# Performer attention with two MoE layers: a block's slot, the last PSUM sums and the splitting of float64 weights

## The chip, the cores and the metric

The kernel runs on one NeuronCore of a Trainium2 chip. The metric is the device time of one execution in microseconds, from launch to the last store.

## The reference

Inputs: q, k, v of 4 batches x 8 heads x 576 tokens x 64, omega of 128 x 64, and the weights of two layers, w_a, w_b (512 x 1536), w_out (1536 x 512), w_in2 (512 x 2048) and w_out2 (2048 x 512). The weights arrive as float64.

```python
def phi(x):
    proj = np.einsum('bhsd,md->bhsm', x, omega)
    h = proj - np.sum(x * x, axis=-1, keepdims=True) / 2.0
    return np.exp(h - np.max(h, axis=-1, keepdims=True)) / np.sqrt(m)
...
num = np.einsum('bhsm,bhmd->bhsd', q_p, kv)
den = np.einsum('bhsm,bhm->bhs', q_p, z)[..., None] + 1e-06
x = (num / den)                      # 2304 tokens x 512
...
x = ((x @ w_a) * (x @ w_b)) @ w_out  # first layer
h = np.maximum(x @ w_in2, 0.0)
out = (h * h) @ w_out2               # second layer
```

## The kernel before

Every matrix operand is kept as a pair of fp32r values, a high half and a low half, and each product is three matmuls (`TERMS`: high x high, high x low, low x high). The work has three stages, all in one program.

**Attention and phase A (0 to some 655 us).** Lanes of attention steps (`k_lane`, `q_lane`) and the passes of the first layer (`a_units`) are emitted interleaved. For each of 12 blocks f of 128 hidden columns, a pass multiplies x by w_a and w_b (L636) and, after `gs`, by w_out (L661). The weights are made once, in the first passes: `get_w` loads a pair of w_a and w_b as 128 x 1024 float64 values, that is two int32 words each, into one of two buffers `raw`; `get_wo` does so for a 128 x 512 piece of w_out and stores the finished pair to `wo_d`, from which later passes load it. `load_split` keeps a load waiting for a few steps, then calls `split` (L166). There are 12 splits of each size. In `split`, `up` is the upper word and `u` the lower one of each float64:

- ACT scales the upper word as a float into `a` (L179), and turns the top 16 bits of the lower word into a number in place, in `raw` (L180).
- DVE makes the float32 value p, cut to its upper mantissa bits, out of `a` by a shift, a mask and the sign (L183, L187). ACT casts p to the high half (L191).
- DVE joins the remaining bits in `raw` (L192), takes the exponent of p into `a` (L196) and multiplies the two into the low half (L200).

`raw` has two buffers, `a` and `p` (the pool `cut`) one each.

**The first half of the second layer (some 655 to 825 us).** It is done by a scheme of seven products on 2 x 2 blocks (`in_step`), whose squared relu h*h goes to DRAM, `s_d[g]`, in four blocks a11, a12, a21, a22 (numbers 0 to 3) for each of three groups g of 768 tokens.

**The second half (`out_phase`, some 825 us to the end).** For each group seven products (`OUTS`) are summed in PSUM: in order X of a11, Y of a22, X of a12, W of a22, Y of a11, W of a12, Y of a21, each with its own block of weights, each over eight steps k. `sq_load` brings a block from `s_d` into one of five slots, `SQ_AT`: 0 is in area AB, 1 and 2 in area F, 3 and 4 in area T. F is also where the stage before keeps its results until they are stored; T is opened over that stage's areas. `prep(n)` makes the operand of step n, `LA` = 4 steps ahead: ACT casts the block to the high half (L1091), DVE subtracts for the low half (L1092, W<-F, W<-T or W<-AB by the block's slot), and from some products on DVE replaces a block by a sum or difference of two (`tt`, L1076). Five buffers `SOP_AT` in W take the operands in turn. Behind each product the PSUM sums are evicted (L1152 on DVE, L1157 on ACT). The loads just ahead of `out_phase` are issued on one queue in the order of the code:

```python
    sq_load(2, 0, 1)      # slot 2 (in F) <- group 0, block 1 (a12)
    sq_load(3, 0, 2)      # slot 3 (in T) <- group 0, block 2 (a21)
    op_load(T1)
```

In the last product of the last group, the three tiles t of 128 tokens are done one after the other, eight steps each, and each is evicted and stored at once (L1139). All three lie in one PSUM tile [128, 4, 256].

The order of the instructions on each engine is set by a scheduler from dependences, not by the code alone.

Of the kernel before, what the change touches and what calls it, by code (L numbers as in the profile page):

```python
# [8 lines left out]
F32 = mybir.dt.float32  # L9
F32R = mybir.dt.float32r  # L10
I32 = mybir.dt.int32
U32 = mybir.dt.uint32
U16 = mybir.dt.uint16
ACTF = mybir.ActivationFunctionType
ALU = mybir.AluOpType
AXX = mybir.AxisListType.X
# [5 lines left out]
TERMS = ((0, 0), (0, 1), (1, 0))  # L22
# [5 lines left out]
WORD_SCALE = 2.0 ** -111  # L28
# [8 lines left out]
def f32(ap):  # L37
    return ap.bitcast(F32)


def i32(ap):
    return ap.bitcast(I32)
# [3 lines left out]
def kernel(  # L46
# [13 lines left out]
    nc = tc.nc  # L60
# [53 lines left out]
    TH, NG = 384, NT // 768  # L114
    NJ = FB // 2
# [6 lines left out]
    def seg(name, off, *shape):  # L122

        n = 1
        for d in shape:
            n *= d
        t = area[name][:, off // 4:off // 4 + n]
        if len(shape) == 1:
            return t
        names = "abcdef"[:len(shape)]  # L130
        return t.rearrange(
            f"p ({' '.join(names)}) -> p {' '.join(names)}",
            **{c: d for c, d in zip(names[1:], shape[1:])},
        )
# [35 lines left out]
    def split(raw, t):  # L170

        n = raw.shape[1]
        up = raw[:, :, :, 1]
        u = raw[:, :, :, 0]
        a = top["cut"].tile([128, 2, 512], F32, tag="a", name="a")[:, 0:n]
        p = top["cut"].tile([128, 2, 512], F32, tag="p", name="p")[:, 0:n]
        nc.scalar.activation(out=a, in_=f32(up), func=ACTF.Copy, scale=WORD_SCALE)  # L179
        nc.scalar.activation(  # L180
            out=u, in_=raw.bitcast(U16)[:, :, :, 1], func=ACTF.Copy, scale=2.0 ** 7,
        )
        nc.vector.tensor_scalar(  # L183
            out=i32(p), in0=i32(a), scalar1=3, scalar2=0x7FFFF000,
            op0=ALU.logical_shift_left, op1=ALU.bitwise_and,
        )
        nc.vector.scalar_tensor_tensor(  # L187
            out=i32(p), in0=i32(a), scalar=-0x80000000, in1=i32(p),
            op0=ALU.bitwise_and, op1=ALU.bitwise_or,
        )  # L190
        nc.scalar.copy(out=t[:, :, 0, :], in_=p)  # L191
        nc.vector.scalar_tensor_tensor(  # L192
            out=u.bitcast(U32), in0=up.bitcast(U32), scalar=23, in1=u.bitcast(U32),
            op0=ALU.logical_shift_left, op1=ALU.bitwise_or,
        )
        nc.vector.tensor_scalar(  # L196
            out=i32(a), in0=i32(p), scalar1=-0x00800000, scalar2=None,
            op0=ALU.bitwise_and,
        )
        nc.vector.scalar_tensor_tensor(  # L200
            out=t[:, :, 1, :], in0=u.bitcast(U32), scalar=2.0 ** -43, in1=a,
            op0=ALU.mult, op1=ALU.mult,
        )


# [818 lines left out]
    def sq(slot):  # L1024
        return seg(*SQ_AT[slot], NJ, TH)

    def sq_load(slot, g, q_, j0=0, j1=8):
        nc.sync.dma_start(out=sq(slot)[:, j0:j1], in_=s_d[g][:, q_, j0:j1])
# [30 lines left out]
    ISC = 1.0 / W_SCALE  # L1059

    def out_phase():
        slots = {0: 0, 3: 1, 1: 2, 2: 3}
        free = 4
        loaded = {}
        sp1, rr, u1, sp5, c11 = (seg("T", 24576 + 3072 * x, 3, 256) for x in range(5))
        todo = [(g, i, k) for g in range(NG) for i in range(7) for k in range(NJ)]
        maps = [slots]
        for g in range(1, NG):
            m = maps[-1]
            maps.append({0: free, 3: m[3], 1: m[0], 2: m[1]})  # L1070
            free = m[2]
        sops = {}
        LA = len(SOP_AT) - 1

        def tt(o, x, y, op):
            nc.vector.tensor_tensor(out=o, in0=x, in1=y, op=op)  # L1076

        def prep(n):
            g, i, k = todo[n]
            m = maps[g]  # L1080
            a11, a12, a21, a22 = (sq(m[x])[:, k] for x in range(4))
            if i == 4:
                tt(a11, a22, a11, ALU.subtract)
            if i == 5:
                tt(a12, a12, a11, ALU.subtract)
            src = sq(m[OUTS[i][1]])[:, k]
            if n >= len(todo) - NJ:
                sop = seg("W", 43008 + 3072 * k, 2, TH)
            else:
                sop = seg(*SOP_AT[n % len(SOP_AT)], 2, TH)  # L1090
            nc.scalar.copy(out=sop[:, 0], in_=src)  # L1091
            nc.vector.tensor_tensor(out=sop[:, 1], in0=src, in1=f32(sop[:, 0]), op=ALU.subtract)  # L1092
            sops[n] = sop
            if i == 2:
                tt(a22, a21, a22, ALU.add)
            if i == 3:
                tt(a21, a11, a21, ALU.subtract)
            if g + 1 < NG and k == NJ - 1:
                nm = maps[g + 1]
                if i == 0:  # L1100
                    sq_load(nm[0], g + 1, 0)
                if i == 4:
                    sq_load(nm[3], g + 1, 3)
                if i == 5:
                    sq_load(nm[1], g + 1, 1)
                    sq_load(nm[2], g + 1, 2)

        def block(p, n, b, k, t, fresh):
            w = seg(*OP_AT[b][k], 2, 256)
            for s_, m_ in TERMS:  # L1110
                nc.tensor.matmul(  # L1111
                    p[:, t], lhsT=sops[n][:, s_, 128 * t:128 * t + 128], rhs=w[:, m_, :],
                    start=(fresh and k == 0 and t % 2 == 0 and (s_, m_) == TERMS[0]),
                    stop=(k == NJ - 1 and t > 0 and (s_, m_) == TERMS[-1]),
                    skip_group_check=True,
                )

        for n in range(LA):
            prep(n)
        ps = {}  # L1120
        for n, (g, i, k) in enumerate(todo):
            c, _, b = OUTS[i]
            if k == 0 and (c not in ps or ps[c][1] != g):
                tag = f"Y{g % 2}" if c == "Y" else c
                ps[c] = (psb.tile([128, 4, 256], F32, tag=tag, name=f"o{c}"), g)
                fresh = True
            elif k == 0:
                fresh = False
            p = ps[c][0]
            if n + LA < len(todo):  # L1130
                prep(n + LA)
            if n >= len(todo) - NJ:
                if k < NJ - 1:
                    continue
                for t in range(3):
                    for x in range(NJ):
                        block(p, n - NJ + 1 + x, b, x, t, False)
                    for o, d1 in ((sp1, 0), (sp5, 1)):
                        nc.vector.scalar_tensor_tensor(  # L1139
                            out=o[:, t], in0=p[:, t], scalar=ISC, in1=o[:, t],  # L1140
                            op0=ALU.mult, op1=ALU.add,
                        )
                        store(g, 1, d1, o, (t,))
                return
            for t in range(3):
                block(p, n, b, k, t, fresh)
            if k < NJ - 1:
                continue
            p = p[:, 0:3]

            def stt(o, sc, y):
                nc.vector.scalar_tensor_tensor(  # L1152
                    out=o, in0=p, scalar=sc, in1=y, op0=ALU.mult, op1=ALU.add
                )

            if i == 0:
                nc.scalar.mul(out=sp1, in_=p, mul=ISC)  # L1157
            elif i == 1:
                stt(rr, -ISC, sp1)
            elif i == 2:  # L1160
                nc.scalar.mul(out=c11, in_=p, mul=ISC)
                store(g, 0, 0, c11)
            elif i == 3:
                nc.scalar.mul(out=sp5, in_=p, mul=ISC)
                tt(sp5, rr, sp5, ALU.add)
            elif i == 4:
                stt(u1, ISC, rr)
            elif i == 5:
                stt(u1, ISC, u1)
                store(g, 0, 1, u1)  # L1170
            else:
                stt(sp1, ISC, sp1)
                store(g, 1, 0, sp1)
                stt(sp5, ISC, sp5)
                store(g, 1, 1, sp5)
# [67 lines left out]
    lanes, n = start_lanes()  # L1243
# [15 lines left out]
    side, n_side, done, u = iter(()), 0, 0, 0  # L1259
# [60 lines left out]
    psb = ctx.enter_context(tc.tile_pool(name="psb", bufs=1, space=bass.MemoryType.PSUM))  # L1320
# [25 lines left out]
    rst.close()  # L1346
    open_area("Q", 9216, F32R, "right")
    open_area("T", 39936, F32, "right")
    sq_load(2, 0, 1)
    sq_load(3, 0, 2)  # L1350
    op_load(T1)
    op_load(T2)
    op_load(B22)
    op_load(T3)
    out_phase()


# [31 lines left out]
```

## Time and profile before

| | us |
|---|---|
| median of 3 runs | 1023.91 |
| lowest and highest | 1022.79, 1028.66 |
| the profiled execution | 1023.56 |
| its span, first to last instruction | 1021.8 |
| PE, DVE, ACT, POOL busy | 987.2, 679.0, 551.3, 29.7 |

The profile is of one execution. PE is the matmul engine and PEld its weight loads, DVE the vector engine, ACT the scalar engine, SPq the queue that issues transfers. A group is given as "line engine operation out<-in", with the shape of one, its count, the busy time in us and the mean of one in ns; behind the last bar stands the idle time just before, with what ended it. PEclk is the granted clock of TensorE as a share of its full 2.4 GHz. Names such as T, F, W, AB are the areas in which the operands lie; oX, oY, oW are PSUM sums of `out_phase`, ps_p those of the attention's projections.

### The profile page before, as it was taken

How to read it: one execution, taken by the hardware profiler on the slowest of the kernel's cores; microseconds unless marked ns; L12 is line 12 of the kernel's file. 1: busy time of each engine (PE TensorE's matmuls, PEld its weight loads, DVE VectorE, ACT ScalarE, POOL GpSimd, SP SyncE). 2: the span in 40 equal slices, each digit the busy share in tenths (PEclk: the TensorE clock that was granted, in tenths of full speed). 3: DMA queues.
4: the chain of work that ended last, by engine and by line, in shares of the span. 5: the costliest groups of instructions: out<-in, count | busy, mean ns of one | idle time of the engine just before them, and what ended most of it. 6: DMA issues, size and time to landing. Idle time of an engine off the chain costs nothing.

```text
span 1021.8 us, 17357 instructions
## 1 busy us (share of the span) xinstructions
PE 987.2 (97%) x6337; PEld 902.3 (88%) x6337; DVE 679.0 (66%) x1651; ACT 551.3 (54%) x1305; POOL 29.7 (3%) x54
## 2 busy tenths in 40 slices
PE   4899999999999999999999999999999998999997
PEld 3789989999988887788888888899999998999997
DVE  4798796575655544443434999978776448697893
ACT  4986766564445553243333545767766544545561
POOL 3100101000000000000000000000000000000000
PEclk9999999999999999999999999999999998999999
DMA  6855865663452111232115999157595599514201
GB/s 170 243 154 181 271 224 155 195 215 115 140 170 70 55 55 55 67 94 72 54 61 165 328 329 330 42 175 241 172 293 197 208 407 419 204 56 167 82 17 47
DMA packets 110501, 171.07 MB, mean 167 GB/s; under 512 B 27728, under 2 KB 83536, under 8 KB 107856
## 3 DMA queue, kind: packets, MB, share of 16 engines
q1 hardware_dynamic: 108880, 168.39, 49.3%
q0 software_dynamic: 1536, 1.58, 0.6%
q8 instruction: 50, 0.82, 0.3%
q14 instruction: 35, 0.29, 0.1%
HBM read 120.13 MB, written 49.81 MB: 166 GB/s over the span
## 4 chain that ended last, share of the span: by engine, by line
PE 86%; DVE 6%; DMA 4%; ACT 2%; issue 1%; SPq 1%; DVEq 0%; ACTq 0%
PE abw L636 18%; PE y L661 12%; PE pY L966 10%; PE oY L1111 8%; PE ab L636 7%; PE oX L1111 5%; PE oW L1111 5%; PE pW L966 5%; PE ps_n L508 3%; PE pX L966 2%; PE ps_kv L450 2%; PE ps_p L378 2%; PE ps_p L312 2%; PE ps_qt L501 1%; DMA raw<-in_moe_w_b_dram 1%; DMA raw<-in_moe_w_out_dram 1%
## 5 line engine op out<-in xcount | busy, mean ns | idle before, releaser
L636 PE MATMUL abw<-x_all,W 128*128 128x512 f32 x576 | 146.6, 398 | 0.0
L661 PE MATMUL y<-gs,wo 128*128 128x256 f32 (+1 forms) x720 | 142.8, 336 | 0.0
L636 PEld LDWEIGHTS abw<-x_all,W 128*128 128x128 f32 x576 | 105.5, 189 | 19.2
L661 PEld LDWEIGHTS y<-gs,wo 128*128 128x128 f32 x720 | 109.6, 190 | 9.5
L636 PE MATMUL ab<-x_all,W 128*128 128x256 f32 x576 | 88.1, 294 | 0.0
L636 PEld LDWEIGHTS ab<-x_all,W 128*128 128x128 f32 x576 | 75.8, 191 | 0.7
L636 PE MATMUL abw<-x_mid,W 128*128 128x512 f32 x288 | 73.1, 400 | 0.0
L636 PEld LDWEIGHTS abw<-x_mid,W 128*128 128x128 f32 x288 | 52.2, 189 | 9.8
L385 DVE CUSTOM_DVE_ANT_0 c<-ps_p,c 128x128 f32<-128x128 f32 x152 | 37.8, 287 | 32.5 <-ACT c L383 32.0
L1091 ACT CAST W<-F 128x384 fp32r<-128x384 f32 x72 | 36.1, 512 | 41.4 <-PE oX L1111 21.5
L1111 PE MATMUL oW<-W 128*128 128x256 f32 x432 | 52.8, 283 | 0.0
L1111 PEld LDWEIGHTS oW<-W 128*128 128x128 f32 x432 | 52.3, 192 | 0.0
L1092 DVE TENSOR_TENSOR W<-F,W 128x384 fp32r<-128x384 f32 x72 | 39.4, 557 | 15.2 <-ACT W L1091 14.9
L742 ACT CAST gs<-a_s 128x256 fp32r<-128x256 f32 x84 | 33.2, 408 | 26.7 <-DVE a_s L741 26.4
L1111 PE MATMUL oX<-W 128*128 128x256 f32 x324 | 42.7, 295 | 4.1 <-DVE W L1092 4.1
L966 PE MATMUL pY<-W,M 128*128 128x384 f32 x240 | 45.9, 335 | 0.7 <-ACT AB L674 0.7
L383 ACT COPY c<-ps_p 128x256 f32<-128x256 f32 x76 | 27.1, 370 | 35.7 <-PE ps_p L378 35.2
L1111 PEld LDWEIGHTS oX<-W 128*128 128x128 f32 x324 | 42.0, 204 | 4.3 <-DVE W L1092 4.3
L636 PE MATMUL ab<-x,W 128*128 128x256 f32 x288 | 43.4, 290 | 0.5 <-DVE x L576 0.4
L1091 ACT CAST W<-T 128x384 fp32r<-128x384 f32 x56 | 28.7, 512 | 27.7 <-PE oY L1111 12.8
L966 PEld LDWEIGHTS pY<-W,M 128*128 128x128 f32 x240 | 41.9, 188 | 1.2 <-ACT AB L674 1.2
L1111 PE MATMUL oY<-W 128*128 128x256 f32 x324 | 40.9, 284 | 1.7 <-DVE T L1139 1.7
(193 smaller groups left out, 2108.0 us busy)
## 6 DMA issues: line engine op xcount, KB each, us to landing
wo<-wo_d SPq DMA_DIRECT2D x60, 512.0 KB, 3.5
s_d<-F SPq DMA_DIRECT2D x24, 768.0 KB, 6.1
raw<-in_moe_w_out_dram SPq DMA_DIRECT2D x32, 256.0 KB, 4.6
raw<-in_moe_w_in_dram SPq DMA_DIRECT2D x16, 512.0 KB, 6.7
W<-wo_d SPq DMA_DIRECT2D x4, 2048.0 KB, 14.7
F<-s_d SPq DMA_DIRECT2D x5, 1536.0 KB, 7.9
raw<-in_moe_w_a_dram SPq DMA_DIRECT2D x12, 512.0 KB, 5.0
raw<-in_moe_w_b_dram SPq DMA_DIRECT2D x12, 512.0 KB, 6.2
```

Of the source, the lines that this page charges most:

```text
L312: nc.tensor.matmul(ps[:, 2 * x:2 * x + 2].rearrange("p h m -> p (h m)"), lhsT=s, rhs=OMZ.rearrange("p h m -> p (h m)"), start=True, stop=True,
L378: nc.tensor.matmul(ps[:, x].rearrange("p a m -> p (a m)"), lhsT=self.s[:, x, o:o + 128], rhs=OM.rearrange("p a m -> p (a m)"), start=True, ...
L383: nc.scalar.copy(out=c, in_=ps[:, :, 1, :])
L385: nc.vector.tensor_tensor_reduce(out=c[:, x, :], in0=ps[:, x, 0, :], in1=c[:, x, :], scale=1.0, scalar=3.0e38, op0=ALU.add, op1=ALU.min, a ...
L508: nc.tensor.matmul(pn[:, x, :], lhsT=t["qT"][:, x % 2 * len(g) + x // 2, :], rhs=kv[:, x % 2, :], start=True, stop=True,)
L636: nc.tensor.matmul(ps, lhsT=wv[:, s_, kc, :], rhs=x[..., kc, m_, :], start=(kc == 0 and (s_, m_) == TERMS[0]), stop=(kc == KC - 1 and (s_, ...
L661: nc.tensor.matmul(y_part(pi, f, c), lhsT=wo[pi, f][:, s_, c * 128:(c + 1) * 128], rhs=g[:, m_, :],  start=(f == f0 and (wide or c % 2 == ...
L742: nc.scalar.copy(out=g[:, 0, c], in_=a_s)
L966: nc.tensor.matmul(p, lhsT=w[:, s_, 128 * kk:128 * kk + 128], rhs=y[:, ai, kk, m_, :], start=(c not in seen and kk == 0 and (s_, m_) == TE ...
L1091: nc.scalar.copy(out=sop[:, 0], in_=src)
L1092: nc.vector.tensor_tensor(out=sop[:, 1], in0=src, in1=f32(sop[:, 0]), op=ALU.subtract)
L1111: nc.tensor.matmul(p[:, t], lhsT=sops[n][:, s_, 128 * t:128 * t + 128], rhs=w[:, m_, :], start=(fresh and k == 0 and t % 2 == 0 and (s_, m ...
```

## The change

It has three parts. In `split`, p becomes the float32 value with all its mantissa bits, the last three of them joined from the lower word; the low half is p less the high half, so the weights are float32 words cut off from float64. ACT's conversion of the lower word and DVE's mask of the exponent are gone. In `out_phase`, blocks 1 (a12) and 2 (a21) trade slots, and their first loads trade places: block 1 now goes to T, by the first of the two. In the last group, the sums Y lie in two PSUM tiles: tiles t = 0 and 2 of 128 tokens in one, t = 1 in the other, and an eviction of all three is made of two instructions.

```diff
-        up = raw[:, :, :, 1]
-        u = raw[:, :, :, 0]
...
-        nc.scalar.activation(out=a, in_=f32(up), func=ACTF.Copy, scale=WORD_SCALE)
-        nc.scalar.activation(
-            out=u, in_=raw.bitcast(U16)[:, :, :, 1], func=ACTF.Copy, scale=2.0 ** 7,
-        )
+        nc.scalar.activation(out=a, in_=f32(raw[:, :, :, 1]), func=ACTF.Copy, scale=WORD_SCALE)
         nc.vector.tensor_scalar(
-            out=i32(p), in0=i32(a), scalar1=3, scalar2=0x7FFFF000,
+            out=i32(p), in0=i32(a), scalar1=3, scalar2=0x7FFFFFF8,
             op0=ALU.logical_shift_left, op1=ALU.bitwise_and,
         )
...
+        nc.vector.scalar_tensor_tensor(
+            out=p.bitcast(U32), in0=raw[:, :, :, 0].bitcast(U32), scalar=29,
+            in1=p.bitcast(U32), op0=ALU.logical_shift_right, op1=ALU.bitwise_or,
+        )
         nc.scalar.copy(out=t[:, :, 0, :], in_=p)
-        nc.vector.scalar_tensor_tensor(
-            out=u.bitcast(U32), in0=up.bitcast(U32), scalar=23, in1=u.bitcast(U32),
-            op0=ALU.logical_shift_left, op1=ALU.bitwise_or,
-        )
-        nc.vector.tensor_scalar(
-            out=i32(a), in0=i32(p), scalar1=-0x00800000, scalar2=None,
-            op0=ALU.bitwise_and,
-        )
-        nc.vector.scalar_tensor_tensor(
-            out=t[:, :, 1, :], in0=u.bitcast(U32), scalar=2.0 ** -43, in1=a,
-            op0=ALU.mult, op1=ALU.mult,
+        nc.vector.tensor_tensor(
+            out=t[:, :, 1, :], in0=p, in1=f32(t[:, :, 0, :]), op=ALU.subtract
         )
...
-        slots = {0: 0, 3: 1, 1: 2, 2: 3}
+        slots = {0: 0, 3: 1, 1: 3, 2: 2}
...
+        def tiles_of(p, t):
+            return p[0][:, t] if len(p) == 1 or t % 2 == 0 else p[1][:, 0]
...
-                    p[:, t], lhsT=sops[n][:, s_, 128 * t:128 * t + 128], rhs=w[:, m_, :],
+                    tiles_of(p, t), lhsT=sops[n][:, s_, 128 * t:128 * t + 128], rhs=w[:, m_, :],
...
+                        tags = ["Y0", "Y1"] if g == NG - 1 else [f"Y{g % 2}"]
+                    ps[c] = ([psb.tile([128, 4, 256], F32, tag=x, name=f"o{c}") for x in tags], g)
...
-    sq_load(2, 0, 1)
-    sq_load(3, 0, 2)
+    sq_load(3, 0, 1)
+    sq_load(2, 0, 2)
```

The lines of the changed program are shifted: L1092 of before is L1081 there, L1076 is L1065, L1152 is L1157, and in `split` L183, L187, L192 and L200 are answered by L177, L181, L185 and L190.

First place: DVE in `out_phase`, group 0, from the operands of the first Y product (W<-AB is the end of the X product, W<-F of before the Y product) to those of the second X product and its eviction of the Y sums (T<-oY). Before:

```order
L1092 TENSOR_TENSOR W<-AB,W 128x384 x3
L1092 TENSOR_TENSOR W<-F,W 128x384 x8
L1076 TENSOR_TENSOR F<-T,F 128x384 x4
L1152 SCALAR_TENSOR_TENSOR T<-oY,T 128x768
L1076 TENSOR_TENSOR F<-T,F 128x384 x4
L1076 TENSOR_TENSOR T<-AB,T 128x384 x2
L1092 TENSOR_TENSOR W<-F,W 128x384 x5
```

Now:

```order
L1081 TENSOR_TENSOR W<-AB,W 128x384 x3
L1081 TENSOR_TENSOR W<-F,W 128x384 x8
L1081 TENSOR_TENSOR W<-T,W 128x384 x4
L1157 SCALAR_TENSOR_TENSOR T<-oY,T 128x768
L1081 TENSOR_TENSOR W<-T,W 128x384 x4
L1065 TENSOR_TENSOR F<-F 128x384 x8
L1081 TENSOR_TENSOR W<-F,W 128x384
L1065 TENSOR_TENSOR F<-AB,F 128x384
```

The subtractions for the second X product (W<-F before, W<-T now) have moved ahead of the sums of two blocks, four of them ahead of the eviction; the eight sums now stand behind them in one piece, ahead of the subtraction for the next product.

Second place: DVE in the attention's opening, at the split of the second pair of weights (p, a, raw, W are of the split; ps_x, ps_p, ps_n, den of the attention). Before:

```order
L183 TENSOR_SCALAR p<-a 128x1024
L526 TENSOR_TENSOR x_all<-ps_x,x_all 128x256
L187 SCALAR_TENSOR_TENSOR p<-a,p 128x1024
L316 TENSOR_REDUCE nm<-ps_p 128x4
L192 SCALAR_TENSOR_TENSOR raw<-raw 128x1024
L196 TENSOR_SCALAR a<-p 128x1024
L482 TENSOR_SCALAR den<-ps_n 128x4
L200 SCALAR_TENSOR_TENSOR W<-raw,a 128x2x512
```

Now:

```order
L177 TENSOR_SCALAR p<-a 128x1024
L515 TENSOR_TENSOR x_all<-ps_x,x_all 128x256
L305 TENSOR_REDUCE nm<-ps_p 128x4
L181 SCALAR_TENSOR_TENSOR p<-a,p 128x1024
L305 TENSOR_REDUCE nm<-ps_p 128x4
L185 SCALAR_TENSOR_TENSOR p<-raw,p 128x1024
L305 TENSOR_REDUCE nm<-ps_p 128x4
L471 TENSOR_SCALAR den<-ps_n 128x4
L305 TENSOR_REDUCE nm<-ps_p 128x2
L474 RECIPROCAL den<-den 128x4
L190 TENSOR_TENSOR W<-p,W 128x2x512
```

Four instructions on wide operands remain of five, the last user of `raw` is the third of them, and five small ones of the attention stand between the second and the last, three of them between the join and the subtraction that reads ACT's high half.

Third place: PE at the end of the program, the last product's three groups of 24 matmuls; the number behind oY tells PSUM tiles apart. Before:

```order
L1111 MATMUL oY_10249<-W_100 128x256 x9
L1111 MATMUL oY_10249<-Q_8784,W_100 128x256 x12
L1111 MATMUL oY_10249<-M_6452,W_100 128x256 x3
L1111 MATMUL oY_10249<-W_100 128x256 [waits DVE_49]
L1111 MATMUL oY_10249<-W_100 128x256 x8
L1111 MATMUL oY_10249<-Q_8784,W_100 128x256 x12
L1111 MATMUL oY_10249<-M_6452,W_100 128x256 x3
L1111 MATMUL oY_10249<-W_100 128x256 [waits DVE_49]
```

Now:

```order
L1111 MATMUL oY_10201<-W_100 128x256 x9
L1111 MATMUL oY_10201<-Q_8736,W_100 128x256 x12
L1111 MATMUL oY_10201<-M_6404,W_100 128x256 x3
L1111 MATMUL oY_10202<-W_100 128x256 x9
L1111 MATMUL oY_10202<-Q_8736,W_100 128x256 x12
L1111 MATMUL oY_10202<-M_6404,W_100 128x256 x3
L1111 MATMUL oY_10201<-W_100 128x256 [waits DVE_49]
L1111 MATMUL oY_10201<-W_100 128x256 x8
```

The second group has no wait for DVE any more; the third, which writes the first group's PSUM tile again, keeps one, now a group of 24 matmuls behind the eviction for which it waits.

## Rows read from the trace of the kernel before

**Rows 1.** The page, busy time of each engine, share of the span, instructions.
```profile
PE 987.2 (97%) x6337; PEld 902.3 (88%) x6337; DVE 679.0 (66%) x1651; ACT 551.3 (54%) x1305; POOL 29.7 (3%) x54
```

**Rows 2.** Stretches: from:to, length, busy time of each engine, granted clock, DMA share, GB/s.
```profile
core 0: us, PE busy (x) PEld busy (x) DVE busy (x) ACT busy (x) POOL busy (x), PEclk, DMA share, GB/s
25.00:60.00 35.00, 30.63 (x210) 26.26 (x209) 28.66 (x55) 32.20 (x85) 4.50 (x7) 1.00 0.76 226
25.00:230.00 205.00, 196.36 (x1514) 185.02 (x1512) 157.45 (x377) 146.57 (x363) 18.90 (x31) 1.00 0.66 205
230.00:625.00 395.00, 394.38 (x2143) 329.06 (x2142) 219.09 (x713) 172.92 (x468) 2.34 (x4) 1.00 0.40 130
844.40:848.70 4.30, 0.23 (x2) 0.02 (x1) 4.27 (x9) 1.18 (x3) 0.00 (x0) 0.91 1.03 434
848.70:855.20 6.50, 6.48 (x32) 6.48 (x33) 5.65 (x12) 1.53 (x3) 0.00 (x0) 0.54 1.00 426
```

**Rows 3.** The chain that ended last, 835 to 860 us: start, us, what.
```profile
835.73 8.67 PE oY L1111 x70
...
844.43 0.04 DVE T L1152
...
845.30 1.96 DVE F L1076 x4
847.26 0.94 DVE T L1076 x2
848.20 0.48 DVE W L1092
...
848.72 11.28 PE oX L1111 x70
```

**Rows 4.** Timeline and transfers (KB each, us from issue to landing), 828 to 844 us.
```profile
828.76 1.23 SPq L1028 DMA_DIRECT2D T<-s_d  x1
...
T<-s_d SPq DMA_DIRECT2D x1, 1536.0 KB, 10.9
...
843.42 1.34 ACT L1091 CAST W<-F 128x384 fp32r<-128x384 f32 x3 [4.00 <-DMA F<-s_d]
...
835.82 0.42 SPq L1019 DMA_DIRECT2D W<-wo_d  x1
...
W<-wo_d SPq DMA_DIRECT2D x1, 2048.0 KB, 12.5
```

**Rows 5.** Waits of PE's loads, 1003 to 1019 us: total, times, longest.
```profile
PEld oY L1111 <- DVE T L1139: 2.1, 2, 1.1
```

**Rows 6.** The chain that ended last, 1000 us to the end.
```profile
1006.88 2.89 PE oY L1111 x24
...
1010.14 0.42 DVE T L1139
...
1010.61 3.15 PE oY L1111 x24
```

**Rows 7.** Groups of instructions by shape, in the split (550 to 790 us for the last).
```profile
L180 ACT ACTIVATE raw<-raw 128x1024 int32<-128x1024 uint16 x12 | 14.1, 1172 | 2.2 <-DMA raw<-in_moe_w_b_dram 2.2
L180 ACT ACTIVATE raw<-raw 128x512 int32<-128x512 uint16 x12 | 8.3, 691 | 1.7 <-DMA raw<-in_moe_w_out_dram 1.7
L191 ACT CAST W<-p 128x1024 fp32r<-128x1024 f32 x12 | 12.6, 1049 | 3.5 <-DVE p L187 3.5
L192 DVE SCALAR_TENSOR_TENSOR raw<-raw 128x1024 uint32<-128x1024 uint32 x12 | 14.7, 1221 | 1.8 <-ACT raw L180 1.8
L196 DVE TENSOR_SCALAR a<-p 128x1024 int32<-128x1024 int32 x12 | 8.4, 698 | 0.1
L196 DVE TENSOR_SCALAR a<-p 128x512 int32<-128x512 int32 x12 | 5.1, 423 | 0.1
L200 DVE SCALAR_TENSOR_TENSOR W<-raw,a 128x1024 fp32r<-128x1024 uint32 x12 | 14.6, 1217 | 0.1
...
L893 DVE TENSOR_TENSOR M<-AB,M 128x1024 fp32r<-128x1024 f32 x9 | 11.0, 1221 | 1.4 <-ACT M L890 1.4
```

**Rows 8.** Operations of line 312: least, median and longest ns, first and last start.
```profile
L312 PEld LDWEIGHTS ps_p<-OMZ,S x104: 186/190/338, 15.7 to 134.2; 128*128 128x128 f32 x104
L312 PE MATMUL ps_p<-OMZ,S x104: 377/379/797, 15.7 to 134.4; 128*128 128x256 f32 x104
```

More of the change, by code (lines that the diff above doesn't have):

```diff
@@ L1106, in prep, with parts_of @@
                     sq_load(nm[2], g + 1, 2)
+        def tiles_of(p, t):
+            return p[0][:, t] if len(p) == 1 or t % 2 == 0 else p[1][:, 0]
+        def parts_of(p, *aps):
+            if len(p) == 1:
+                return [(p[0][:, 0:3], *aps)]
+            return [
+                (p[0][:, 0:3:2], *(x[:, 0:3:2] for x in aps)),
+                (p[1][:, 0:1], *(x[:, 1:2] for x in aps)),
+            ]
         def block(p, n, b, k, t, fresh):
@@ L1111, in block @@
                 nc.tensor.matmul(
-                    p[:, t], lhsT=sops[n][:, s_, 128 * t:128 * t + 128], rhs=w[:, m_, :],
-                    start=(fresh and k == 0 and t % 2 == 0 and (s_, m_) == TERMS[0]),
-                    stop=(k == NJ - 1 and t > 0 and (s_, m_) == TERMS[-1]),
+                    tiles_of(p, t), lhsT=sops[n][:, s_, 128 * t:128 * t + 128], rhs=w[:, m_, :],
+                    start=(
+                        fresh and k == 0 and (t % 2 == 0 or len(p) == 2)
+                        and (s_, m_) == TERMS[0]
+                    ),
+                    stop=(k == NJ - 1 and (t > 0 or len(p) == 2) and (s_, m_) == TERMS[-1]),
                     skip_group_check=True,
@@ L1122, in out_phase @@
             c, _, b = OUTS[i]
[L1123 to L1128, printed above, removed]
+            if k == 0:
+                fresh = c not in ps or ps[c][1] != g
+                if fresh:
+                    if c != "Y":
+                        tags = [c]
+                    else:
+                        tags = ["Y0", "Y1"] if g == NG - 1 else [f"Y{g % 2}"]
+                    ps[c] = ([psb.tile([128, 4, 256], F32, tag=x, name=f"o{c}") for x in tags], g)
             p = ps[c][0]
@@ L1139, in out_phase @@
                         nc.vector.scalar_tensor_tensor(
-                            out=o[:, t], in0=p[:, t], scalar=ISC, in1=o[:, t],
+                            out=o[:, t], in0=tiles_of(p, t), scalar=ISC, in1=o[:, t],
                             op0=ALU.mult, op1=ALU.add,
@@ L1148, in out_phase @@
                 continue
-            p = p[:, 0:3]
             def stt(o, sc, y):
-                nc.vector.scalar_tensor_tensor(
-                    out=o, in0=p, scalar=sc, in1=y, op0=ALU.mult, op1=ALU.add
-                )
+                for x, o_, y_ in parts_of(p, o, y):
+                    nc.vector.scalar_tensor_tensor(
+                        out=o_, in0=x, scalar=sc, in1=y_, op0=ALU.mult, op1=ALU.add
+                    )
             if i == 0:
-                nc.scalar.mul(out=sp1, in_=p, mul=ISC)
+                nc.scalar.mul(out=sp1, in_=p[0][:, 0:3], mul=ISC)
             elif i == 1:
@@ L1160, in out_phase @@
             elif i == 2:
-                nc.scalar.mul(out=c11, in_=p, mul=ISC)
+                nc.scalar.mul(out=c11, in_=p[0][:, 0:3], mul=ISC)
                 store(g, 0, 0, c11)
             elif i == 3:
-                nc.scalar.mul(out=sp5, in_=p, mul=ISC)
+                nc.scalar.mul(out=sp5, in_=p[0][:, 0:3], mul=ISC)
                 tt(sp5, rr, sp5, ALU.add)
```

1 line of the change is left out of this document (removed).

## The prediction

> **What bounds the kernel now.** I read the page's line of totals first: PE is busy 987.2 of 1021.8 us, 97%, and DVE, the next, 66% [rows 1]. So a microsecond counts only where PE stands idle, or runs below full speed, and some 35 us is all that waits can give. The table of stretches says where that is [rows 2]. In each row the reader compares PE's busy time with the length of the stretch, and looks at the granted clock. From 25 to 230 us, where the attention's leftovers, the weights' splitting and phase A's first passes run together, PE lacks 205.0 - 196.36 = 8.6 us, half of it before 60 us (35.0 - 30.63 = 4.4), where ACT is busy for 32.2 of 35 us. From 230 to 625 us it lacks 0.6 us: nothing that the change does there to ACT or DVE can be felt. Around 844.4 us it lacks 4.1 us, and in the 6.5 us behind that the granted clock is 0.54 of full speed.
>
> The chain of waits tells that hole link by link [rows 3]. PE ends the first Y product at 844.4, and starts the second X product at 848.7. In between the chain lies on DVE: the rest of an eviction, four sums F<-T, two sums T<-AB, and only then the subtraction (0.48 us) that gives PE its next operand. DVE takes its instructions in order, and the sums stand ahead of the subtraction because ACT, which casts the operand first, got its source late: the transfer into F, issued behind one into T, landed at 843.4 (the cast's row: 4.00 us of idle ACT ended by "DMA F<-s_d") [rows 4]. The one into T was issued at 828.8 and took 10.9 us, so it had landed by 839.7.
>
> At the end, PE's loads wait twice for DVE, 1.1 us each time [rows 5]: between the three tiles of the last product it stands until DVE has read the tile that lies in the same PSUM tile as the next one. 24 matmuls take 2.89 us where nothing waits, and the chain shows an eviction of 0.42 us between two groups [rows 6].
>
> **The change, part by part.** *The slot.* The block of the second X product comes by the first transfer, into T, and that of a later sum by the second, into F. The second X product's first operands can then be cast from 839.7 on, 4.7 us before PE asks for them. In the new order, DVE's subtractions W<-T stand ahead of the eviction and ahead of the sums, so PE finds them done at 844.4: the 4.1 us go. With them goes the low clock that followed: the 70 matmuls of that product took 11.28 us, the 70 of the Y product before it 8.67 [rows 3], a difference of 2.6; the clock's row gives 6.5 x 0.46 = 3.0 [rows 2]. I take 2.8. What is late next: the sums for the third block now wait for F (843.4). Eight F<-F at 1.96 / 4 = 0.49 us are 3.9 us, and in the new order they stand between the subtraction for the product's last operand and that for the first of the next product. The former waits for a buffer that comes free with the product's third operand, 3 x 1.08 us behind 844.4 at 847.65; a cast and a subtraction (0.48 us each) later it is 848.6, behind the sums 852.5, and 853.0 to 853.2 when the next product's first operand is done. PE asks for it 8.65 us after 844.4, at 853.05. I cost that at nothing; it is 0.2 us if nothing covers it. The weights of the next product (T1) were issued at 835.8 and took 12.5 us, so they have landed at 848.3 [rows 4]; PE will want them at 853.05 instead of 860: covered. In the two later groups the same swap puts one load into the other area; there the loads lie far ahead of their use. Nothing. **-4.1 and -2.8.**
>
> *The tail.* With tiles 0 and 2 in one PSUM tile and tile 1 in another, the next group's matmuls have no eviction to wait for; the third group does go back to the first tile, but that was read while the second group ran (2.89 us against two evictions of 0.42). The last eviction and stores stay. The two waits go [rows 5]: **-2.1**. For it, two evictions of the last group are cut into two instructions each; an eviction of 256 columns takes 0.42 us [rows 6], so even if each cut cost a whole one of these, it would be 0.84 us. PE works on the next product meanwhile, with four operands prepared: at nothing.
>
> *The weights.* Per pair of w_a and w_b ACT loses one conversion of 1172 ns, per w_out one of 691 ns [rows 7]: 12 x 1.172 + 12 x 0.691 = 22.4 us, of the 146.6 that ACT is busy from 25 to 230 us. DVE loses the mask for the exponent, 698 ns and 423 ns: 12 x 1.121 = 13.5 of 157.5 us. The join of the words is again a scalar_tensor_tensor of the same width over uint32 (1221 ns then and now), and the last product (1217 ns) becomes a subtraction, whose nearest row, 128x1024 from float32 into fp32r elsewhere in the kernel, also has 1221 [rows 7]. Those two trades are at nothing. The raw slot is now read last by the third DVE instruction and not by the fifth, so the next weights' transfer may be issued earlier; and the cut tile that ACT writes first is free after DVE's second instruction. What is added is a wait: the low half now needs ACT's high half. Behind it on DVE stand the attention's reductions and small divisions, and in the new order they stand partly ahead of it, as the rows of the order show.
>
> What that gives PE, no row tells; so bounds. The most is all of its idle time from 25 to 230, 8.6 us. The least is a loss: in the opening stretch, where PE idles for ACT and DVE, two pairs are split, and if each low half there waits out a whole cast of the high half (1049 ns), that is 2 x 1.05 = 2.1 us lost. I take half of the 8.6, **-4.3**, since half of that idle time lies before 60 us where ACT is busy 92% of the stretch, and 15% of its work over the 205 us goes; the rest sits behind transfers and PE's own chain.
>
> The page named PE by its matmuls' busy time. In the Trainium skill, Perfetto Trace Analysis, section Identifying the Most-Contended Engine, it is said that matmul busy time is a poor measure since matmuls are pipelined, and that the busy time of weight loads tells the room. By it the sum would be some 6 us lower (third rival). The trace speaks against it here: a matmul of ps_p holds PE for 379 ns and its load for 190 [rows 8], so loads idle half the time there while PE has no gap.
>
> The sum: 4.1 + 2.8 + 2.1 + 4.3 = 13.3 us. The profiled execution took 1023.56 us, 0.35 below the median of the runs (1023.91): 1023.56 - 13.3 = **1010.3 us**. With the bounds of phase A: 1006.0 to 1016.7.
>
> **The rivals.** *Phase A gives nothing.* For it: from 60 to 230 us PE is busy 196.36 - 30.63 = 165.7 of 170 us, and a scheduler has set all engines' order anew, so a wait may only move. Against: ACT's load in the opening. Time: 1023.56 - 9.0 = 1014.6, up to 1016.7 with the loss above. 20%.
>
> *The hole moves.* DVE's eight F<-F sums (3.9 us) come at once and in one place; if ACT's casts there are late too, PE waits at the first W product as it did at the second X product, and the clock drops again. Then the 6.9 us come back: 1017.2. For it: the sums are queued ahead of a subtraction as before. Against: they start some 4 us before PE needs it, with four operands prepared. 8%.
>
> *PE has more room than its busy time shows.* Going by the loads, PE is idle 205.0 - 185.0 = 20.0 us between 25 and 230 [rows 2]; half of it gone would give 1023.56 - 9.0 - 10.0 = 1004.6. 7%, by the row against it above.
>
> *Slower: the low half's new wait.* ACT's queue is long there, and each low half waits in DVE's queue for a cast behind other ACT work, with PE's evictions behind it. If PE loses a whole cast at each of the splits, 1.05 us per pair and half of that per w_out, it is 12 x 1.05 + 12 x 0.53 = 19 us: 1023.56 - 9.0 + 19 = 1033.6. It decides from 9.0 / 24 = 0.38 us per split; below that the kernel isn't slower. For it: DVE is in order. Against: between the subtraction and the join DVE has other instructions, and PE has a lead. 4%.
>
> *It doesn't do what it says*: the tail still waits, and the hole stays (the cast's source was in time, but ACT's queue wasn't). Then only phase A's 4.3: 1019.3. 3%.
>
> **How the numbers follow.** The forecast has 58%, with 1006.0 to 1014.6 as its own range. For 8 in 10 the range takes in the rival of nothing from phase A, that of the moved hole with its clock, and the third, since the sizes within each are rough: 1004 to 1018.5. About 0.5%, 5.1 us, is what a measurement of this kernel can tell: faster means below 1018.8. Forecast, first and third rival and nearly all of the second lie there: 0.58 + 0.20 + 0.07 + 0.05 = 0.90, of which I give 0.02 away for what I have not thought of. Within it: 0.09; slower: 0.03.
>
> **What would show it.** Right: from 825 us on no wait of PE for W by DVE above 0.5 us and a clock of 1.00 behind the Y product; the second X product in 8.4 to 8.7 us; no wait of the last loads for T; ACT's busy time lower by 22 us, DVE's by 13; PE's idle time between 25 and 230 at 3 to 6 us. Wrong: a wait for DVE at the first W product, an idle time of 9 us or more before 230, or DVE waiting about 1 us for ACT's cast at each low half, with PE behind it.

## The result, and the profile after

The changed kernel takes 1014.05 us (median of 6 runs, 1010.27 to 1016.17); before took 1024.14 in the runs beside it. The ratio is 0.9894, 95% interval 0.9867 to 0.9922: 10.9 us less by the ratio, 10.1 by the two medians. The forecast was 13.3 us less, 1010.3, with 1004 to 1018.5 as its range. The profiled execution took 1015.39 us, its span is 1013.6.

The page's totals answer to [rows 1]. PE's busy time is the same, ACT has lost 19.2 us and DVE 11.2; the prediction's 22.4 and 13.5 us were sums of durations. The page counts stretches in which an instruction ran, and back-to-back instructions overlap a little there; that this is all of the difference is not shown:

```profile
PE 985.9 (97%) x6337; PEld 901.7 (89%) x6337; DVE 667.8 (66%) x1629; ACT 532.1 (52%) x1281; POOL 29.2 (3%) x54
```

The chain of waits behind 826 us answers to [rows 3] (start, us, what):

```profile
826.00 8.64 PE oX L1111 x72
...
836.52 8.64 PE oY L1111 x70
845.16 8.64 PE oX L1111 x72
853.80 8.64 PE oW L1111 x72
```

The Y product ends at 845.16 and the second X product starts there, where it stood until 848.72 before. It takes 8.64 us, not 11.28: the low clock is gone with the wait. The first W product follows without a gap too. At the end there is no row for a wait of the loads on T ([rows 5] had 2.1 us); what is left from 822 us on for PE's loads is the wait ahead of the first Y product, which before has as well:

```profile
PEld oY L1111 <- ACT W L1080: 1.5, 1, 1.5
PEld oY L1111 <- DVE W L1081: 0.3, 1, 0.3
```

So the last stage, from the first X product to the last instruction, takes 1013.6 - 826.0 = 187.6 us. Before it was 1021.8 - 825.22 = 196.6, by this row of before's chain:

```profile
825.22 8.64 PE oX L1111 x72
```

That is 9.0 us, the 4.1, 2.8 and 2.1 of the sum. What is missing is all in front of it: the first X product starts 0.8 us later than before, where 4.3 us earlier was forecast. (These are single executions. In the traces of e1, e3 and e4 below, whose order up to that product is before's, it starts at 826.33 to 826.66, so before's 825.22 is an early one.) The stretches say more (to be read beside [rows 2]):

```profile
core 0: us, PE busy (x) PEld busy (x) DVE busy (x) ACT busy (x) POOL busy (x), PEclk, DMA share, GB/s
25.00:60.00 35.00, 31.91 (x211) 27.11 (x212) 26.51 (x53) 27.93 (x84) 4.59 (x8) 1.00 0.72 214
150.00:153.00 3.00, 1.14 (x9) 0.73 (x7) 1.04 (x4) 2.42 (x5) 0.00 (x0) 1.00 1.05 353
153.00:158.00 5.00, 5.00 (x29) 4.97 (x30) 1.12 (x6) 1.31 (x5) 0.00 (x0) 0.66 0.65 219
25.00:230.00 205.00, 198.70 (x1524) 188.12 (x1525) 148.14 (x355) 129.86 (x346) 18.96 (x32) 0.99 0.65 201
```

PE's idle time from 25 to 230 us fell from 8.6 to 6.3. But of the 3 us from 150 on PE is idle for 1.9, and in the next 5 the granted clock is 0.66: 5 x 0.34 = 1.7 us of work lost. Outside this range PE is also busy for less: 10.81 us of the first 25 (11.72 before; its wait for the load of omega takes 3.9 us instead of 3.3), and 13.81 us from 640 to 655 (14.22 before). That accounts for the 0.8 us: 2.3 - 1.7 - 0.9 - 0.4 = -0.7. Of the six runs, two had a mean granted clock of 1.000 and 0.999 and took 1010.27 and 1011.27 us; the other four, the profiled one among them, had 0.998 and took 1013.07 to 1016.17.

In the kernel before, the same stretches have holes of 1.6 and 0.4 us, of which PE waits 1.5 us for DVE (xh, L486), and the clock stays at 1.00:

```profile
150.00:153.00 3.00, 1.41 (x10) 1.01 (x9) 2.88 (x5) 2.97 (x6) 0.00 (x0) 1.00 0.56 154
153.00:158.00 5.00, 4.61 (x38) 4.40 (x38) 4.24 (x17) 2.92 (x10) 0.00 (x0) 1.00 0.92 300
```

So the hole as such is not new; its cause is. In the changed kernel the chain of waits tells where it comes from:

```profile
145.23 0.45 PE ps_t L346 x4
...
145.70 0.38 SPq L326
...
146.12 5.32 DMA raw<-in_moe_w_b_dram
...
151.60 1.12 ACT a L176
152.72 0.16 ACT x L564
...
152.93 1.18 PE ab L625 x7
```

Read from the bottom: PE waits for a cast of x on ACT; that stands behind ACT's scaling `a` of the last pair of weights; this waits for w_b; and w_b's transfer was issued at 146.12, behind a load of wo and one of k (L326), which waited one after the other on the same queue for PE. Its partner w_a had gone out at 142.78. Both went out earlier than in the kernel before (153.27 and 153.71), but ACT's scaling of the pair has moved up as well, ahead of the cast. Another thing shows in the groups of the split (0 to 250 us):

```profile
L190 DVE TENSOR_TENSOR W<-p,W 128x1024 fp32r<-128x1024 f32 x12 | 14.7, 1221 | 3.2 <-ACT W L189 3.1
...
L190 DVE TENSOR_TENSOR wo<-p,wo 128x512 fp32r<-128x512 f32 x12 | 8.3, 690 | 5.5 <-ACT wo L189 5.4
```

DVE stands for 3.1 + 5.4 = 8.5 us ahead of the subtractions, until ACT has cast the high half: most of the 13.5 us that the missing mask gave it.

### The profile page after: what moved, and what is told of

It reads as the page before. It is cut to its first block, busy times and chain, and to the rows that moved or that the text cites. A ratio compares the mean times of both kernels' runs of the same rounds, so it can differ in the third digit from the quotient of the medians.

```text
span 1013.6 us, 17323 instructions
## 1 busy us (share of the span) xinstructions
PE 985.9 (97%) x6337; PEld 901.7 (89%) x6337; DVE 667.8 (66%) x1629; ACT 532.1 (52%) x1281; POOL 29.2 (3%) x54
## 4 chain that ended last, share of the span: by engine, by line
PE 82%; DVE 8%; DMA 4%; ACT 3%; issue 1%; SPq 1%; ACTq 0%; DVEq 0%
PE abw L625 13%; PE y L650 11%; PE pY L955 10%; PE ab L625 9%; PE oY L1111 8%; PE oW L1111 5%; PE oX L1111 5%; PE pW L955 5%; PE ps_n L497 3%; PE ps_p L301 3%; PE pX L955 2%; PE ps_kv L439 2%; PE ps_p L367 2%; DMA raw<-in_moe_w_b_dram 2%; PE ps_qt L490 1%
## 5 line engine op out<-in xcount | busy, mean ns | idle before, releaser
L625 PEld LDWEIGHTS abw<-x_all,W 128*128 128x128 f32 x576 | 105.5, 189 | 19.2
L1081 DVE TENSOR_TENSOR W<-F,W 128x384 fp32r<-128x384 f32 x72 | 39.6, 562 | 11.6 <-ACT W L1080 11.0
L1080 ACT CAST W<-T 128x384 fp32r<-128x384 f32 x56 | 28.5, 513 | 30.2 <-PE oY L1111 10.9
L625 PEld LDWEIGHTS ab<-x,W 128*128 128x128 f32 x288 | 39.2, 198 | 1.5 <-ACT x L564 1.5
L1111 PEld LDWEIGHTS oY<-W 128*128 128x128 f32 x324 | 39.8, 192 | 0.1
```

What stands on the lines that cost most here:

```text
L625: nc.tensor.matmul(ps, lhsT=wv[:, s_, kc, :], rhs=x[..., kc, m_, :], start=(kc == 0 and (s_, m_) == TERMS[0]), stop=(kc == KC - 1 and (s_, ...
L1111: nc.tensor.matmul(tiles_of(p, t), lhsT=sops[n][:, s_, 128 * t:128 * t + 128], rhs=w[:, m_, :], start=(fresh and k == 0 and (t % 2 == 0 or ...
```

## The experiments

Times are medians, compared with runs of the kernel before on the same chip (1025.08 beside e1 to e4, 1025.21 beside e5 to e8, 1024.23 beside e9 and e10, 1024.40 beside the last two). Since these differ, gains are compared by the ratios: 0.001 is 1.02 us.

**The three parts apart.** e1 is the changed kernel with before's `split`. e2 is the kernel before with the new `split` alone. e3 and e4 are the kernel before with one of the other parts:

```diff
# e3
-        slots = {0: 0, 3: 1, 1: 2, 2: 3}
+        slots = {0: 0, 3: 1, 1: 3, 2: 2}
...
-    sq_load(2, 0, 1)
-    sq_load(3, 0, 2)
+    sq_load(3, 0, 1)
+    sq_load(2, 0, 2)
# e4
-                tag = f"Y{g % 2}" if c == "Y" else c
+                        tags = ["Y0", "Y1"] if g == NG - 1 else [f"Y{g % 2}"]
```

> Before's splitting of the weights, with the new slot and the two PSUM tiles. Theory: the weights' part gave nothing, all of the gain is in the last stage: the stage in front as before (the first X product starts at 825.2 us), the last stage as in the changed kernel (187.6 us to the end): span 1012.8, time about 1014.6, level with the changed kernel within 2 us, and no low clock near 155 us. Rival: the weights' part gave its 4.3 us and the rest less: then this kernel takes 1018 or more.

> The new splitting alone, slot and PSUM tile as before. Theory: within 2 us of before (about 1024), PE's idle time from 25 to 230 us about 6 us instead of 8.6, and this given back by a stretch of low clock behind a hole near 151 us. Rival: 4 us faster, 1019 to 1020.

> The slot alone. By the sum: 4.1 us of wait and 2.8 of low clock go: 1024.1 - 6.9 = 1017.2; the two waits of 1.1 us at the end stay. Rival: the wait moves to the next W product and the clock falls there: 1022 or more.

> The two PSUM tiles alone. By the sum: 2.1 us, 1022.0; the wait of 4.1 us ahead of the second X product and the low clock stay. Rival: the two evictions cut in two cost what the tail gives: 1024.

| | us | ratio to before | 95% interval |
|---|---|---|---|
| e1 slot and tail | 1015.81 | 0.9907 | 0.9889 to 0.9925 |
| e2 weights alone | 1022.40 | 0.9969 | 0.9957 to 0.9982 |
| e3 slot alone | 1019.33 | 0.9939 | 0.9917 to 0.9962 |
| e4 tail alone | 1023.93 | 0.9984 | 0.9966 to 1.0002 |

The last stage can be read off each trace, from the first X product to the end of the span. The first rows of the chain there, of e1, e3 and e4, and the second X product of e4:

```profile
826.51 8.64 PE oX L1122 x72
```
```profile
826.66 8.64 PE oX L1111 x72
```
```profile
826.33 8.64 PE oX L1122 x72
...
849.82 10.15 PE oX L1122 x70
```

With spans of 1014.1, 1016.5 and 1019.6 us the stage takes 187.6, 189.8 and 193.3 us, against 196.6 before. The slot is worth 6.8 us (6.9 by the sum), and the tail 2.2 on top of it (2.1 by the sum). In e4, 1.1 of its 3.3 us are not the tail's: the second X product behind the same hole took 10.15 us instead of 11.28, the low clock having ended sooner. The timings of e3 and e1 agree with the traces. That of the tail alone does not tell: 1023.93 is its rival's number, and the interval holds both nothing and the 2.1 us; its ten runs lie between 1020.86 and 1027.92. What speaks for the tail is the stage in the traces, and e1 against e3. In e3 the loads' waits at the end are still there:

```profile
PEld oY L1111 <- DVE T L1139: 2.1, 2, 1.1
```

The weights' part gave 3.2 us alone (1.8 to 4.4), and beside the others 0.9907 - 0.9894, about 1.3 us, within the uncertainty of both (some 3.4 us either way). So the part gives something, which speaks against "nothing", and most likely less than the 4.3 of the forecast, which the timings alone do not rule out. Its trace (e2) has the hole and the low clock near 150 us too. So has that of e4, although it has before's split, and on PE, DVE and ACT up to 970 us the same instructions in the same order as the kernel before. Its holes are those of before, 1.6 and 0.4 us, and yet behind them:

```profile
153.00:158.00 5.00, 4.61 (x27) 4.59 (x26) 3.21 (x11) 1.65 (x4) 0.00 (x0) 0.66 0.91 292
```

Whether a hole of this size costs clock thus differs between executions of one order; the 1.7 us are what it cost in the profiled one.

**The hole near 151 us.** Two experiments move one row each in the changed kernel, with an order-only edge between two instructions; every row of PE and DVE stays where it was. In e5 the k load and a load of wo are issued behind the last w_b (ACT's scaling then moves up two rows); in e6 ACT's scaling of that pair stands one row later, behind the cast of x, and w_b is as late as before. In short (the names stand for the instructions; the first is put behind the second):

```diff
# e5
+    tc.add_manual_dep(k_load[10], w_b_load[11], NoSync)
+    tc.add_manual_dep(wo_load[6], w_b_load[11], NoSync)
# e6
+    tc.add_manual_dep(a_scale[11], x_cast[3], NoSync)
```

> The changed kernel with one difference: the transfer of the last w_b is issued right behind that of its w_a, ahead of a load of k (and of one of wo) that waits for PE. Theory: in the changed kernel w_b lands at 151.4 us behind that load, ACT's scaling of it holds up the cast of x behind it, PE stands 0.57 + 1.29 us and then runs at half clock until 157.7. Here w_b lands near 149.5, the second hole is under 0.5 us and the clock stays at 1.00: 1.1 + 1.8 us less than the changed kernel's 1014.05, about 1011. Rival: the stage is bound by PE's other work, and the time stays within 1 us of 1014.

> The changed kernel with one difference: on ACT the scaling of the last pair stands one row later, behind the cast of x that PE waits for; w_b is as late as before. Theory: the 1.29 us of waiting for the cast go and with them the low clock from 154 to 157.7: about 1011. Rival: the pair's split, now later, is what PE waits for next, or the clock falls for the 0.57 us that stay: 1013 to 1014.

Measured: e5 1011.92 us (0.9872, 0.9853 to 0.9891), e6 1012.19 (0.9869, 0.9851 to 0.9888); 2.3 and 2.6 us better than the changed kernel by the ratios, each within the uncertainty of such a difference, 3.4 us. In the traces the first X product starts at 822.96 and 823.61, 3.0 and 2.4 us earlier than in the changed kernel. ACT's rows of e6 (start, us, engine, line), w_b issued at 145.86:

```profile
151.18 0.27 ACT L569 CAST x<-ps_xt 128x128 fp32r<-128x128 f32 x1 [0.31 <-PE ps_xt L563]
151.40 1.14 ACT L181 ACTIVATE a<-raw 128x1024 f32<-128x1024 f32 x1
```

and its stretch, to be held against that of the changed kernel above:

```profile
150.00:153.00 3.00, 2.31 (x17) 1.87 (x16) 1.14 (x5) 2.38 (x5) 0.00 (x0) 1.00 1.03 347
153.00:158.00 5.00, 5.00 (x45) 5.00 (x43) 3.26 (x21) 4.08 (x14) 0.00 (x0) 1.00 0.58 210
```

PE is idle for 0.7 us of the three, and the clock stays. So w_b's landing hurts through ACT's order alone: w_b is not wanted yet, but what ACT does with it stands ahead of something that PE wants. From 25 to 230 us the two save 0.5 and 0.8 us of PE's idle time, and the rest is the low clock; their times are level with those two runs of the changed kernel that did without it (1010.27 and 1011.27). Without the hole the weights' part is worth 0.9907 - 0.9870, about 3.8 us.

**What of the weights' part counts.** e7 and e8 start from e1 and leave out one instruction of before's `split` each.

```diff
# e7
-        nc.scalar.activation(
-            out=u, in_=raw.bitcast(U16)[:, :, :, 1], func=ACTF.Copy, scale=2.0 ** 7,
-        )
# e8
-        nc.vector.tensor_scalar(
-            out=i32(a), in0=i32(p), scalar1=-0x00800000, scalar2=None,
-            op0=ALU.bitwise_and,
-        )
```

> The kernel of e1 (before's splitting with slot and tail) without ACT's conversion of the lower words, so that the low halves get wrong bits. Theory: what the weights' part gains in the opening comes from ACT's 22.4 us: PE's idle time from 25 to 60 us falls from 4.3 to about 3, the whole 2 to 3 us below e1 (1015.8), about 1013. Rival: it comes from DVE's five instructions becoming four: then this one stays within 1 us of 1015.8.

> The kernel of e1 without DVE's mask of the exponent, so that the low halves have a wrong scale. Theory: DVE's 13.5 us are not what PE waits for: idle time from 25 to 60 us stays near 4.3, time within 1 us of 1015.8. Rival: they are: 2 us less, 1013.5.

Measured: e7 1013.69 us (0.9885, 0.9867 to 0.9903), e8 1009.22 (0.9849, 0.9827 to 0.9872). Against e1 that is 2.3 and 5.9 us, the former within its uncertainty of 2.6. e7 came as expected. e8's theory, that DVE's 13.5 us are not what PE waits for, fell, and by more than its rival named: they are worth at least as much as ACT's 22.4. The stretches of e7, then of e8:

```profile
25.00:60.00 35.00, 32.70 (x222) 28.10 (x221) 30.21 (x59) 29.09 (x83) 4.56 (x8) 1.00 0.76 227
25.00:230.00 205.00, 200.47 (x1543) 188.95 (x1542) 160.03 (x385) 131.16 (x346) 18.61 (x32) 1.00 0.67 207
```
```profile
25.00:60.00 35.00, 33.50 (x231) 29.35 (x229) 27.90 (x54) 32.16 (x89) 4.87 (x8) 1.00 0.76 226
25.00:230.00 205.00, 201.81 (x1562) 191.56 (x1560) 150.54 (x372) 148.84 (x376) 18.88 (x32) 1.00 0.67 210
```

In e8 ACT is as busy as before (32.16 of 35 us), and yet PE is idle for only 1.5 us of the opening, where before had 4.4: ACT's busy share does not tell what it costs PE. The chain of waits tells more. In the kernel before all of PE's waits from 25 to 60 us end with ACT, 4.3 us in all, but from 30.5 to 36.9 us the chain runs over DVE and its split, the mask (L196) in it, and from there to ACT's next scaling; the conversion (L180) is not on it:

```profile
35.02 0.60 DVE a L196
35.62 0.07 DVE den L482
35.69 1.20 DVE W L200
36.89 0.02 issue
36.91 0.67 ACT a L179
```

In e8, without the mask, the conversion is on the chain:

```profile
32.42 1.18 ACT raw L180
```

Either instruction alone leaves PE less idle time (4.5 and 3.2 us from 25 to 230) than the change does, which drops both (6.3). Both kernels got another order from the scheduler, too, so a part of the difference is the order's.

**The low half's wait.** That the change adds a wait of DVE for ACT was the next suspect. In e9 the low half is p less p, and nothing waits for the cast. In e10 ACT casts p before the last bits are joined, and the join goes to `a`:

```diff
# e9
-            out=t[:, :, 1, :], in0=p, in1=f32(t[:, :, 0, :]), op=ALU.subtract
+            out=t[:, :, 1, :], in0=p, in1=p, op=ALU.subtract
# e10
+        nc.scalar.copy(out=t[:, :, 0, :], in_=p)
         nc.vector.scalar_tensor_tensor(
-            out=p.bitcast(U32), in0=raw[:, :, :, 0].bitcast(U32), scalar=29,
+            out=a.bitcast(U32), in0=raw[:, :, :, 0].bitcast(U32), scalar=29,
             in1=p.bitcast(U32), op0=ALU.logical_shift_right, op1=ALU.bitwise_or,
         )
-        nc.scalar.copy(out=t[:, :, 0, :], in_=p)
         nc.vector.tensor_tensor(
-            out=t[:, :, 1, :], in0=p, in1=f32(t[:, :, 0, :]), op=ALU.subtract
+            out=t[:, :, 1, :], in0=a, in1=f32(t[:, :, 0, :]), op=ALU.subtract
         )
```

> The changed kernel, with the low half made as p less p instead of p less the high half (it becomes zero, so the product lacks it): same instructions and shapes, but DVE no longer waits for ACT's cast. Theory: in the changed kernel DVE stood 3.1 us ahead of the twelve wide subtractions and 5.4 us ahead of the twelve narrow ones for that cast, 8.5 of the 13.5 us that the missing mask had given back; without it the weights' part gives as much as the mask alone did in e8 (1009.2): 1008 to 1010. Rival: those waits are idle time that costs nothing, and what e8 showed came from the order it got: then 1012 to 1014.

> The changed kernel, but ACT casts the high half from p before the last three bits are joined, and DVE's join writes into the tile a, from which the subtraction then reads: nothing is left out, and the cast runs beside the join instead of behind it. Theory: DVE's waits for the cast fall from 8.5 us to 2 or less, and the time to 1009 to 1011, below the changed kernel (1014.05). Rival: a is held until the last instruction again, ACT's next scaling waits for it, and nothing is won: 1013 to 1015.

Measured: e9 1013.47 us (0.9899, 0.9880 to 0.9917), a miss; e10 1010.55 (0.9867, 0.9848 to 0.9885), as expected. In e10 DVE's waits for the cast are down to 2.1 us, and the price that the rival named is there and as large: ACT's next scaling waits for the subtraction (L190), 1.4 + 0.6 us on the wide form and 3.0 + 2.6 us on the narrow one, 7.6 us in all. So a wait of DVE was traded for one of ACT, and the time of e10 does not tell what the former is worth:

```profile
L190 DVE TENSOR_TENSOR W<-a,W 128x1024 fp32r<-128x1024 f32 x12 | 14.6, 1216 | 0.1
L176 ACT ACTIVATE a<-raw 128x1024 f32<-128x1024 f32 x12 | 13.8, 1152 | 3.6 <-DMA raw<-in_moe_w_b_dram 1.7 <-DVE W L190 1.4 <-DVE wo L190 0.6
...
L190 DVE TENSOR_TENSOR wo<-a,wo 128x512 fp32r<-128x512 f32 x12 | 8.2, 687 | 2.5 <-ACT wo L185 2.1
L176 ACT ACTIVATE a<-raw 128x512 f32<-128x512 f32 x12 | 8.1, 675 | 6.0 <-DVE W L190 3.0 <-DVE wo L190 2.6 <-DMA raw<-in_moe_w_out_dram 0.3
```

e9's trace has a hole of 1.2 us at 147.4, of the same kind as that at 151, with the clock at 1.00 behind it: ACT's scaling (ACT idle for 2.18 us until w_b landed), two casts and a copy stand ahead of the cast of x:

```profile
145.91 1.15 ACT L176 ACTIVATE a<-raw 128x1024 f32<-128x1024 f32 x1 [2.18 <-DMA raw<-in_moe_w_b_dram]
...
148.30 0.27 ACT L564 CAST x<-ps_xt 128x128 fp32r<-128x128 f32 x1
```

So e11 puts that scaling behind the cast, as in e6 (here the scheduler moved some rows behind it on all engines as well).

```diff
+    tc.add_manual_dep(a_scale[10], x_cast[2], NoSync)
```

> The kernel of e9 (low half p less p, no wait of DVE for ACT's cast) with the scaling of the last pair but one put behind the cast of x on ACT, as in e6: in e9 PE stood 1.2 us at 147.4 for that cast. Theory: e9 missed its number because of that hole alone; without it 1012.2, and if the rest of the order is as good as in e10, 1010 to 1011, at least 1 us below e5 and e6 (1012), which have the wait and no hole. Rival: it stays at 1012 or above: then DVE's waits for the cast are not worth a microsecond, and e10's gain has another cause.

Measured: 1012.57 us (0.9875, 0.9858 to 0.9891), the rival's number: level with e5 and e6 (0.9872, 0.9869), which have the wait. By the timings, DVE's 8.5 us of waiting for the cast are worth less than can be told, and the theory of the wait is not borne out. e9, whose ACT and PE rows also came in another order, does not settle it either. The 0.0008 between e11 and e10 is within the noise. Why the change leaves PE more idle time than either instruction alone, stays open; the order that the scheduler gave each is the candidate left, and it wasn't isolated.

**A version that beats both.** e12 is e10 with one more row moved (some rows of DVE moved with it): on ACT the first four casts of the first Y product go ahead of the eviction of the X sums, since PE waited 1.3 us for them in every trace.

```diff
+    tc.add_manual_dep(first_eviction, operand_cast[11], NoSync)
```

> The kernel of e10 (1010.55) with one more row moved: on ACT the first four casts of the first Y product stand ahead of the eviction of the first X product; their source lands about 2 us before PE ends that product, and PE waited 1.3 us for the first of them in every kernel so far. Theory: that wait goes, 1009.2. Rival: the eviction, now later, holds up DVE's reader of it or the PSUM tile, or the source lands later than thought: 1010.5 or more.

Measured: 1009.87 us (0.9849, 0.9832 to 0.9866): below before, and its interval lies just under that of the changed kernel. By the ratios that is 1.8 us below e10, within the noise; the new row itself paid little. Its chain:

```profile
822.24 8.63 PE oX L1116 x72
830.87 8.65 PE oY L1116 x72
...
840.42 0.56 DVE W L1086
...
841.03 8.66 PE oX L1116 x70
```

The first wait is gone, and one of 1.3 us has come up at the second X product. On DVE the eviction of the Y sums now stands ahead of all subtractions for that product, where e10 has four of them ahead of it, and DVE waits there until PE has ended the Y product:

```profile
839.55 0.96 DVE L1162 SCALAR_TENSOR_TENSOR T<-oY,T 128x768 f32<-128x768 f32 x1 [4.42 <-PE oY L1116]
```

The stage takes 1009.3 - 822.2 = 187.1 us, 0.5 less than in the changed kernel. A hole has moved, but not the way of the prediction's rival: the F<-F sums come behind it.

## Why the prediction was right, and where it was off

*The slot* was right in its mechanism and its size: 4.1 us of wait and 2.6 us of low clock went (11.28 - 8.64; the sum took 2.8), 6.8 in e3 against 6.9. The low clock is the less certain of the two: behind the same hole it cost 1.5 us in e4's trace. The covers named for it held: the first W product starts as the second X product ends, at 853.80, so neither DVE's eight sums nor the weights T1 were late. The rival of a moved hole did not come; the hole of e12 has another cause.

*The tail* was right: 2.2 us in e1 against e3, 2.1 by the sum. The evictions cut in two cost nothing that PE saw.

*The weights* are the term that was mis-sized: "I take half of the 8.6, **-4.3**". Measured were 1.3 us beside the other parts and 3.2 alone. PE's idle time from 25 to 230 us did fall, but by 2.3 us, to 6.3 (3 to 6 was to be the sign of a right forecast). Near 151 us a wait only moved: PE stood there for 2.0 us before, mostly for DVE, and stands there for 1.9 us now, 1.3 of it for a cast that waits behind work of no urgency; and the low clock behind it took 1.7 us in the profiled execution. The text said that the next weights' transfer "may be issued earlier"; that held for both w_a and w_b of the last pair, but ACT's scaling of the pair moved ahead of the urgent cast, while w_b still stood in the transfer queue behind two loads that wait for PE. The order of that queue has these rows, and the prediction spoke of it for the last stage alone. With the hole closed (e5, e6) the part gives about 3.8 us, near the 4.3. That is luck in part: the reason given was ACT's load in the opening. e7, which frees ACT alone, takes PE's idle time there from 4.3 (e1) to 2.3 us; e8, which frees DVE alone, takes it to 1.5, and DVE's load was not among the reasons.

*The rivals.* "Phase A gives nothing" (1014.6) is nearest to the measured 1014.05, and the reason named there, that a wait may only move, is what the traces show near 151 us; by e2 the part gives more than nothing. "Slower" had the right sign of a cost, DVE does wait 8.5 us for casts, but by the timings of e11 PE hardly feels it. "PE has more room than its busy time shows" was not seen: in the changed kernel the loads are idle for 16.9 us between 25 and 230, and PE for 6.3; in e8, the fastest there, for 13.4 and 3.2. By the rule of the Trainium skill (Perfetto Trace Analysis, Identifying the Most-Contended Engine) the former is the room; the runs won no more than a part of the latter and the low clock. The row that the prediction set against this rule was misread: 379 ns is how long one matmul of ps_p is recorded, but before's chain has four in a row in 0.86 us, 215 ns each, against 190 ns for a load:

```profile
41.93 0.86 PE ps_p L312 x4
```

So matmuls overlap there, and the loads do not idle half of the time. Which of the two measures tells PE's room, no run here settles.

## What to carry to other kernels

When an edit frees engine time where a scheduler sets the order, read the new order of the transfer queue and of the engine that consumes the transfer for what now stands ahead of urgent work: one early scaling on ACT, in front of one cast, was worth 2.3 to 2.6 us by the medians here (2.4 to 3.0 in the traces), about as much as the freed time brought. A transfer that nobody needs yet can still stall the kernel through the engine that takes it up in order. And try the edit's halves alone, and read the chain: that an engine is busy (ACT, 92%) does not say whose instructions stand ahead of the one that the bound engine waits for; in the opening DVE's did as well.

## What was not expected of the hardware

A hole of PE doesn't always cost clock. The 1.3 us ahead of the first Y product is followed by 1.00 in every trace that has it. The 4.1 us ahead of the second X product is followed by a lower clock in before and in e4 (11.28 and 10.15 us for the same 70 matmuls, 8.64 for 72 without the hole). And some 2 us in two pieces near 151 are followed by 0.66 in the changed kernel and in e4, but by 1.00 in before, e1 and e3, although before and e4 have the same instructions in the same order there. Around 647 us, at the end of phase A, PE's wait for the last gated block differs from run to run of nearly the same program: nothing in before's profile, 1.3 us in e2's, with a clock of 0.72 over the 6 us around it. Both may be a part of the spread of 2 to 7 us among runs of one kernel; how large a part is not shown.
